# Gated linear attention and a squared-ReLU MLP: token pairs per partition for chunks ten to twenty-three

## The chip, the cores and the metric

The kernel runs on one core of a Trainium2 chip. The metric is the device time of one execution in microseconds (us); less is better. A core has TensorE (PE, matmuls and transposes), VectorE (DVE), ScalarE (ACT), GpSimd (POOL) and a queue for transfers on SyncE (SP). Each works its own instructions off in a fixed order and waits for the others through semaphores.

## The reference, cut to what matters

```python
batch, n_heads, seq, head_dim = 4, 8, 768, 48          # attention inputs q, k, v, alpha, float32
n_tokens, d_model, d_ff = 3072, 384, 2048

for t in range(S):
    state = alpha[:, :, t, :, None] * state + einsum('bhd,bhe->bhde', k[:, :, t], v[:, :, t])
    y[:, :, t] = einsum('bhd,bhde->bhe', q[:, :, t], state)
x = y.transpose(0, 2, 1, 3).reshape(B * S, H * D)      # 3072 x 384
h = maximum(x @ w_in, 0)
out = (h * h) @ w_out                                  # 3072 x 384, float32
```

alpha lies between 0.8 and 1.

## The kernel before, in words

The 3072 tokens are 24 chunks of 128, six for each batch. A chunk of the attention (below: GLA) is worked in the chunked form. ACT takes the logarithm of alpha (`L_s`), PE multiplies it with a triangle of ones (`utri_b`), which gives the running sum along the tokens, ACT exponentiates the sum with both signs (`A`, `Ainv`), and VectorE forms q·A and k·Ainv (both in `qk_s`). These two are transposed (to `qkT`). PE forms the 128x128 scores per head (`sc`), VectorE masks them while it moves them out of PSUM (`sm`), and PE adds masked scores times v (`vb`) and q·A times the carried state (`sb`). The state `st` stays in PSUM: PE adds k·Ainv times v, VectorE multiplies by the chunk's total decay (`ae_s`), ACT copies it to `sb`. The result `xn` is transposed into `xT_big`.

The MLP follows in 12 groups of chunks, most of them of two chunks. For each group PE forms w_in times x ("moe1", 48 matmuls of 256 columns for two chunks), ACT applies the ReLU (`r`), VectorE squares it (`gT`), and PE multiplies by w_out ("moe2", 16 matmuls of 384 columns per chunk). ACT or VectorE copy the result to `held`, from where it is stored.

Nothing runs in the order of the code. Each step is handed to a planner as an `Op` with an engine or a choice of engines (a dictionary with a duration for each), its dependencies and a priority. `Plan.run` places each on the engine that its durations say will finish it first, `gate` lets a chunk's running sum start only when the MLP's progress is within 3.5 to some 6.5 chunks of it, and the steps are then issued in the order of the planned starts. The order on every engine is therefore fixed when the kernel is built. Between chunks' GLA steps PE has MLP matmuls.

Three kinds of chunk exist:

- Chunks 0 to 3, two at a time (`add_super`): a partition holds two neighbouring tokens, so that the pair's load has runs of 384 bytes.
- Chunks 4 to 11 (`add_chunk` with `s < TURN`): a partition holds one token, and loads have runs of 192 bytes (`add_load`). The totals come from four one-column matmuls and two small ACT instructions (L474, L477).
- Chunks 12 to 23 (`s >= TURN`): the same, but A is written in float32 in another order (`Af`, L467), its last row is sent to `ae_s` by two small transfers on POOL's queue (L484), and q and k are transposed by one DMA on SP's queue (L515) instead of PE. From chunk 14 on, `xn` is transposed by DMA as well (`XTURN`, L414).

In `add_chunk` the products for q and k are one VectorE instruction each (L495 or L498, and L501) over 128 partitions, and POOL casts v to bfloat16 (L443). Chunks are scored one by one up to chunk 7 and two by two from chunk 8 on (`PAIRS`, `add_scores`). Loads are issued on SP's queue in chunk order; ten chunks' buffers (`LB`) are in flight. Results are stored by POOL's queue, the last three by SP's. Until the first moe2, PE also runs idle matmuls on a zero tile (`warm`) in the gaps of the plan.

Of the kernel before, what the change touches and what calls it, by code (L numbers as in the profile page):

```python
# [164 lines left out]
def kernel(  # L165
# [24 lines left out]
    srcs = [(n, a.rearrange("b h (c p) d -> b c p h d", p=P)) for n, a in srcs]  # L190
# [10 lines left out]
    LB = 10  # L201
# [27 lines left out]
    )  # L229
    utri_b = consts.tile([P, 1, P], BF16)  # L230
    nc.vector.tensor_copy(utri_b[:, 0, :], utri_f)
    half_in = consts.tile([P, P], BF16)
# [15 lines left out]
    ones_col = consts.tile([P, 1], BF16)  # L248
    nc.gpsimd.memset(ones_col, 1.0)

# [3 lines left out]
    NBUF = 4  # L254
    TURN = 12
    AE_LAT = 3.6
    L_s = big.tile([P, NBUF, H, DP], BF16)
    nc.gpsimd.memset(L_s[:, :, :, D:], 0.0)
    qk_s = big.tile([P, NBUF, 2, H, DP], BF16)
    qA_s, kI_s = qk_s[:, :, 0], qk_s[:, :, 1]  # L260
    nc.gpsimd.memset(qA_s[:, :, :, D:], 0.0)
    ident_bf = consts.tile([P, P], BF16)
    make_identity(nc, ident_bf)
    nc.gpsimd.memset(kI_s[:, :, :, D:], 0.0)
    ae_s = big.tile([P, NBUF, 2, NP], FP32)
# [26 lines left out]
    LD = 1.05  # L292
# [53 lines left out]
    SRC = dict(srcs)  # L346
    EARLY = 2 * 3
    PAIRS = 8
    XFROM, XTURN = 12, 14
# [4 lines left out]
    EITHER, SLOW = {"DVE": 0.47, "POOL": 0.95}, {"POOL": 0.95}  # L354
    KI_ON = [[EITHER, EITHER], [EITHER, EITHER]]
    ST_PRIO = -12.0
    SUP = [dict() for _ in range(NS)]

    def add_load(s, nm):
        d = C[s]  # L360
        b, c = divmod(s, NCH)
        k = s // 2

        def ld():
            if s % 2 == 0:
                PAIR[k][nm] = loads.tile([P, 2, H, D], FP32, name=nm)
            d[nm] = PAIR[k][nm][:, s % 2]
            pin(nc.sync.dma_start(out=d[nm], in_=SRC[nm][b, c]))
        prev = C[s - LB]["use_" + nm] if s - LB >= 2 * NS else None
        if 0 <= k - LB // 2 < NS:  # L370
            prev = SUP[k - LB // 2]["use_" + nm]
        d["ld_" + nm] = add("DMA", LD if s < 12 else 0.95, ld, prev, lat=2.4)

    PAIR = [dict() for _ in range(NT // 2)]
# [5 lines left out]
    def add_load2(u, nm):  # L380
        d = SUP[u]
        nm, half = nm[:2], nm[2:]
        hs = slice(HH * int(half), HH * int(half) + HH) if half else slice(0, H)

        def ld():
            if nm not in d:
                d[nm] = loads.tile([P, H, 2, D], FP32, name=nm)
            pin(nc.sync.dma_start(out=d[nm][:, hs].rearrange("p h s d -> p h (s d)"), in_=SRC2[nm][0, u][:, hs]))  # L388
        d["ld_" + nm + half] = add("DMA", LD2 / 2 if half else LD2, ld, lat=2.0, at=0.8)

# [8 lines left out]
    def add_tail(s, done, first, g):  # L399
# [23 lines left out]
        xT = add({"ACT": 0.36, "DVE": 0.27} if s < EARLY else "DVE", 0.27, e_xT, p4, prio=-9.0)  # L423
# [3 lines left out]
    def add_chunk(s):  # L427
        d = C[s]
        b, c = divmod(s, NCH)
        i = s % NBUF  # L430
        L, qA, kI, ae = L_s[:, i], qA_s[:, i], kI_s[:, i], ae_s[:, i].rearrange("p j n -> p n j")
        was = C[s - NBUF]
        old = was["end"] if s < 2 * NS + NBUF else None
        g = dict(prio=-10.0 + s * 0.01)
        last = c == NCH - 1
# [3 lines left out]
        ln = d["use_at"] = add("ACT", 0.41, e_ln, d["ld_at"], old or was["p0"], prio=-15.0 if s < EARLY else -5.0)  # L439

        def e_vb():
            d["vb"] = work.tile([P, H, D], BF16, name="vb", bufs=4)
            pin(nc.gpsimd.tensor_copy(d["vb"], d["vt"]))  # L443
        vb = d["use_vt"] = add("POOL", 0.55, e_vb, d["ld_vt"], old or was["end"], prio=-5.0)

        def e_p0():
            pm = d["pm"] = psum(p0, [P, 512], FP32)
            mm(pm[:, 0:HD], lhsT=utri_b[:, 0, :], rhs=L[:, :, 0:D], start=True, stop=True)
            for p in range(NP if s < TURN else 0):
                mm(pm[:, HD + p:HD + p + 1], lhsT=L[:, 2 * p:2 * p + 2, :], rhs=ones_col,  # L450
                   start=True, stop=True)
        p0 = Op("PE", 0.27 if s < TURN else 0.17, e_p0, [ln], takes=GLA_BANKS, lat=0.17, **g)
        p0.gla = s
        d["p0"] = p0

        def split(x, s):
            if s < TURN:
                return x.rearrange("p (h d) -> p h d", h=H)
            return x.rearrange("p (n j d) -> p n j d", n=NP, j=2)

        def e_A():
            if s < TURN:
                d["A"] = work.tile([P, H, D], BF16, name="A")
            else:
                d["Af"] = work.tile([P, 2, D, NP], FP32, name="Af", bufs=2)
                d["A"] = d["Af"].rearrange("p j d n -> p n j d")
            pin(nc.scalar.activation(d["A"], split(d["pm"][:, 0:HD], s), AF.Exp))  # L467

        def e_Ai():
            d["Ai"] = work.tile([P, H, D], BF16, name="Ainv")  # L470
            pin(nc.scalar.activation(d["Ai"], d["pm"][:, 0:HD].rearrange("p (h d) -> p h d", h=H), AF.Exp, scale=-1.0))  # L471

        def e_ae0():
            pin(nc.scalar.activation(ae[0:64, :, 0], d["pm"][0:64, HD:HD + NP], AF.Exp))  # L474

        def e_ae1():
            pin(nc.scalar.activation(ae[64:128, :, 1], d["pm"][64:128, HD:HD + NP], AF.Exp))  # L477
        plan.add(p0)
        a_ = add("ACT", 0.38 if s < TURN else 0.76, e_A, p0, **g)
        ai = add("ACT", 0.38, e_Ai, p0, after(a_), **g)  # L480

        def e_aed():
            for j in range(2):
                pin(nc.gpsimd.dma_start(out=ae_s[HF * j:HF * j + D, i, j], in_=d["Af"][P - 1:P, j]))  # L484
        if s < TURN:
            ae0 = add("ACT", 0.18, e_ae0, p0, after(ai), **g)
            p0.gives = ae1 = add("ACT", 0.19, e_ae1, p0, after(ae0), **g)
        else:
            p0.gives = ai
            ae1 = add("POOL", 1.03, e_aed, a_, lat=AE_LAT, prio=-20.0)  # L490
            ae1.dma = 0.42

        def e_qA():
            if s < TURN:
                pin(nc.vector.tensor_mul(qA[:, :, 0:D], d["qt"], d["A"]))  # L495
            else:
                v4 = "p (n j) d -> p n j d"
                pin(nc.vector.tensor_mul(qA[:, :, 0:D].rearrange(v4, j=2), d["qt"].rearrange(v4, j=2), d["A"]))  # L498

        def e_kI():  # L500
            pin(nc.vector.tensor_mul(kI[:, :, 0:D], d["kt"], d["Ai"]))  # L501
        mq = d["use_qt"] = add("DVE", 0.47 if s < TURN else 0.78, e_qA, a_, d["ld_qt"], old or was["cps"][0], **g)
        mk = d["use_kt"] = add("DVE", 0.47, e_kI, ai, d["ld_kt"], *([old] if old else [was["cps"][1], was.get("ps")]), **g)

        def e_p1q():
            d["pT"] = psum(p1q, [P, 2 * NP, P], BF16)
            for p in range(NP):
                tr(d["pT"][:, p, :], qA[:, 2 * p:2 * p + 2, :], ident_bf)

        def e_p1k():  # L510
            for p in range(NP):
                tr(d["pT"][:, NP + p, :], kI[:, 2 * p:2 * p + 2, :], ident_bf)
        def e_turn():
            d["qkT"] = work.tile([P, 2 * NP, P], BF16, name="qkT")
            pin(nc.sync.dma_start_transpose(out=d["qkT"], in_=qk_s[:, i].rearrange("p x h d -> p (x h d)")))  # L515
        if s < XFROM:
            p1q = plan.add(Op("PE", 0.22, e_p1q, [mq], takes=GLA_BANKS, **g))
            p1k = plan.add(Op("PE", 0.22, e_p1k, [mk, after(p1q)], lat=0.15, **g))

        def e_cp(lo, hi):  # L520
            if lo == 0:
                d["qkT"] = work.tile([P, 2 * NP, P], BF16, name="qkT")
            cast(cpk if lo else cp, d["qkT"][:, lo:hi, :], d["pT"][:, lo:hi, :])
        if s < EARLY:
            cp = add({"ACT": 0.49, "DVE": 0.34}, 0, lambda: e_cp(0, NP), p1q, **g)
            cpk = add({"DVE": 0.34, "ACT": 0.49}, 0, lambda: e_cp(NP, 2 * NP), p1k, after(cp, -9.0), **g)
        elif s < XFROM:
            cp = cpk = add("DVE", 0.61, lambda: e_cp(0, 2 * NP), p1k, was["py_op"], **g)
        else:
            cp = cpk = add("XB", 0.0, e_turn, mq, mk, was["py_op"], lat=2.8)  # L530
            cp.turn = 1.2
        if s < XFROM:
            p1q.gives = cpk

        d.update(cps=[cp, cpk], mk=mk, vb_op=vb, ae1=ae1, kI=kI, ae=ae)
        if s < PAIRS:
            add_scores(s, 1)
            add_back(s)
        elif s % 2:
            add_scores(s - 1, 2)  # L540
            add_back(s - 1)
            add_back(s)
# [429 lines left out]
    for x in DMA_ORDER + [s for s in range(2 * NS, NT) if s not in DMA_ORDER]:  # L972
# [7 lines left out]
        else:  # L980
            for nm, _ in srcs:
                add_load(x, nm)
# [85 lines left out]
```

## Time and profile before

| what | value |
|---|---|
| median of three runs (lowest, highest) | 179.01 us (178.74, 179.09) |
| the profiled execution: its time, its span | 179.8 us, 178.1 us |
| granted TensorE clock in it | 0.999 |
| VectorE: the squares `gT` | 96, 46.1 us busy, mean 514 ns |
| VectorE: the masks `sm` from `sc` and from a bank | 24 of 684 ns, 16 of 681 ns |
| VectorE: q·Af, q·A, k·Ainv | 12 of 854 ns, 8 of 565 ns, 20 of 548 ns |
| ACT: the ReLUs | 96, mean 611 ns |
| ACT: Af, A, Ainv | 12 of 883 ns, 8 of 495 ns, 20 of 514 ns |
| POOL: casts to `vb` of chunks 4 to 23 | 20, 553 ns (507 the usual one) |
| POOL: transfers of `ae_s` and of results | 24 of 511 ns, 17 of 545 ns |
| loads of q, k, alpha, 192 KB each | 24 each, 3.8 to 4.0 us from issue to landing |
| DMA transposes `qkT` and `xT_big` | 12 and 10, 4.4 and 4.0 us to landing |

The profile is one execution. Its span runs from the first to the last instruction, and the time of the execution lies 1.7 us above it. A busy time counts an instruction from start to end; neighbours on an engine can overlap, so the pace of an engine is read from start to start. TensorE's ends are modelled. DMA engines were busy nearly without a break until 150 us. The two last groups' MLP work fills PE from 155 us to 175 us; the last store ends the span.

### The profile page before, as it was taken

The page shows a single profiled execution, that of the slowest core. Times are in us where ns is not written, and L with a number is a line of the kernel's source. Part 1 is how long each engine was busy: PE and PEld are TensorE (multiplying, and loading weights), DVE is VectorE, ACT ScalarE, POOL GpSimd, SP SyncE. Part 2 cuts the span into 40 slices and gives each one's busy share as a digit, 9 for nine tenths or more (in the row PEclk, how much of TensorE's full clock was granted, in tenths as well). Part 3 has the DMA queues.
Part 4 walks back from the last instruction along what each step waited for, and adds up shares of the span by engine and source line. Part 5 has one row for each costly group of instructions (what it writes and reads, how often), then busy time and mean ns, then how long its engine had stood idle before and what let it go on. Part 6 is the DMA issues. An engine that isn't in the chain of part 4 may idle for free.

```text
span 178.1 us, 4801 instructions
## 1 busy us (share of the span) xinstructions
PE 172.0 (97%) x1866; PEld 126.3 (71%) x1867; DVE 124.8 (70%) x256; ACT 122.8 (69%) x263; POOL 53.1 (30%) x95
## 2 busy tenths in 40 slices
PE   7999999999999999999999999899999999999993
PEld 3567684566896788878766786686688867757862
DVE  6699769936799798998986976798248933800600
ACT  4557789456898689979956698874598947522821
POOL 6023467711110211115222233327736080212000
PEclk9999999999999999999999999999999999999999
DMA  5999999999998999988999799999999969232012
GB/s 128 275 271 322 311 352 377 247 194 213 216 185 156 213 184 203 229 176 155 125 214 209 144 209 109 187 193 239 212 204 294 211 162 212 69 91 89 0 44 88
DMA packets 115798, 34.34 MB, mean 193 GB/s; under 512 B 109840, under 2 KB 114064, under 8 KB 115776
## 3 DMA queue, kind: packets, MB, share of 16 engines
q1 hardware_dynamic: 113536, 29.89, 81.5%
q0 software_dynamic: 2240, 4.15, 7.3%
q8 instruction: 14, 0.23, 0.6%
q14 instruction: 8, 0.07, 0.1%
HBM read 25.17 MB, written 4.72 MB: 168 GB/s over the span
## 4 chain that ended last, share of the span: by engine, by line
PE 79%; DMA 7%; DVE 4%; SPq 3%; ACT 3%; issue 1%; ACTq 0%; DVEq 0%
PE bank L273 71%; PE bank L276 4%; SPq L388 3%; DMA qt<-in_q_dram 3%; DMA at<-in_alpha_dram 3%; PE sc L273 2%; PE st L273 2%; DMA kt<-in_k_dram 2%; ACT r L878 1%; DVE sm L570 1%; ACT Af L467 1%; DVE qkT L395 1%; ACT xn L393 0%; DVE sm L763 0%; DVE xT_big L395 0%
## 5 line engine op out<-in xcount | busy, mean ns | idle before, releaser
L273 PE MATMUL bank<-xT_big,w_in_b 128*128 128x256 bf16 (+2 forms) x599 | 72.0, 268 | 0.3 <-ACT r L878 0.2
L273 PE MATMUL bank<-w_out_b,gT 128*128 128x384 bf16 (+2 forms) x400 | 69.8, 319 | 0.0
L878 ACT ACTIVATE r<-bank 128x512 bf16<-128x512 f32 x96 | 57.0, 611 | 13.5 <-PE bank L273 11.5
L886 DVE TENSOR_TENSOR gT<-r 128x512 bf16<-128x512 bf16 x96 | 46.1, 514 | 23.7 <-ACT r L878 23.4
L273 PEld LDWEIGHTS <-w_in_b 128*128 128x128 bf16 x600 | 53.2, 98 | 11.2 <-issue 1.1
L273 PEld LDWEIGHTS <-gT 128*128 128x128 bf16 x400 | 37.1, 98 | 19.4
L443 POOL CAST vb<-vt 128x384 bf16<-128x384 f32 x20 | 11.1, 553 | 58.1 <-DMA vt<-in_v_dram 30.8
L953 ACT COPY held<-bank 128x384 f32<-128x384 f32 x22 | 10.6, 481 | 14.9 <-PE bank L273 14.6
L484 POOL DMA_DIRECT2D ae_s<-Af x24 | 12.2, 511 | 25.4 <-ACT Af L467 22.2
L570 DVE TENSOR_TENSOR sm<-sc,utri_b 128x512 bf16<-128x512 f32 x24 | 15.4, 684 | 2.0 <-PE sc L273 1.8
L273 PEld LDWEIGHTS <-qkT 64*128 64x128 bf16 (+2 forms) x304 | 10.5, 97 | 5.1 <-issue 2.4
L393 ACT CAST xn<-bank 128x384 bf16<-128x384 f32 x24 | 11.1, 485 | 4.4 <-PE bank L273 4.1
L498 DVE TENSOR_TENSOR qk_s<-qt,Af 128x384 bf16<-128x384 f32 x12 | 10.2, 854 | 4.6 <-ACT Af L467 4.6
L438 ACT ACTIVATE L_s<-at 128x384 bf16<-128x384 f32 x20 | 10.6, 543 | 2.7 <-DMA at<-in_alpha_dram 2.7
L961 POOL DMA_DIRECT2D out_dram<-held x17 | 9.2, 545 | 7.9 <-ACT held L953 7.9
L467 ACT ACTIVATE Af<-bank 128x384 f32<-128x384 f32 x12 | 10.6, 883 | 0.9 <-PE bank L273 0.7
L501 DVE TENSOR_TENSOR qk_s<-kt,Ainv 128x384 bf16<-128x384 f32 x20 | 11.0, 548 | 0.0
L395 DVE COPY qkT<-bank 128x1024 bf16<-128x1024 bf16 (+1 forms) x14 | 8.3, 609 | 3.4 <-PE bank L276 3.4
L609 ACT CAST sb<-st 128x384 bf16<-128x384 f32 x16 | 8.0, 499 | 3.9 <-DVE st L604 3.8
L471 ACT ACTIVATE Ainv<-bank 128x384 bf16<-128x384 f32 x20 | 10.3, 514 | 0.0
L570 DVE TENSOR_TENSOR sm<-bank,utri_b 128x512 bf16<-128x512 f32 x16 | 10.2, 681 | 0.0
L604 DVE TENSOR_TENSOR st<-st,ae_s 128x384 f32<-128x384 f32 x16 | 8.9, 557 | 1.7 <-PE st L273 1.7
(71 smaller groups left out, 165.6 us busy)
## 6 DMA issues: line engine op xcount, KB each, us to landing
at<-in_alpha_dram SPq DMA_DIRECT2D x24, 192.0 KB, 4.0
qt<-in_q_dram SPq DMA_DIRECT2D x24, 192.0 KB, 3.8
kt<-in_k_dram SPq DMA_DIRECT2D x24, 192.0 KB, 4.0
vt<-in_v_dram SPq DMA_DIRECT2D x20, 192.0 KB, 3.9
out_dram<-held POOLq DMA_DIRECT2D x17, 192.0 KB, 4.5
wo<-in_moe_w_out_dram SPq DMA_DIRECT2D x4, 768.0 KB, 7.3
wi<-in_moe_w_in_dram SPq DMA_DIRECT2D x4, 384.0 KB, 6.8
wi<-in_moe_w_in_dram SPq DMA_DIRECT2D x2, 768.0 KB, 5.6
```

The lines of the kernel that those rows point to most:

```text
L273: pin(nc.tensor.matmul(*a, **kw))
L393: pin(nc.scalar.copy(out_t, in_t))
L438: pin(nc.scalar.activation(L[:, :, 0:D], d["at"], AF.Ln))
L443: pin(nc.gpsimd.tensor_copy(d["vb"], d["vt"]))
L467: pin(nc.scalar.activation(d["A"], split(d["pm"][:, 0:HD], s), AF.Exp))
L471: pin(nc.scalar.activation(d["Ai"], d["pm"][:, 0:HD].rearrange("p (h d) -> p h d", h=H), AF.Exp, scale=-1.0))
L484: pin(nc.gpsimd.dma_start(out=ae_s[HF * j:HF * j + D, i, j], in_=d["Af"][P - 1:P, j]))
L501: pin(nc.vector.tensor_mul(kI[:, :, 0:D], d["kt"], d["Ai"]))
L570: pin(nc.vector.tensor_mul(d["sm"][:, hh], d["sc"][hh], utri_b.to_broadcast([P, NP, P])))
L878: pin(nc.scalar.activation(box["r"][:, 0:w], box["ph"][:, 0:w], AF.Relu))
L886: pin(nc.vector.tensor_mul(gT[g][:, f0:f0 + per, lo * P:lo * P + n], r, r))
L953: pin(nc.scalar.copy(box["ob"], box["po"]))
```

## The change: token pairs from chunk ten on

Chunks 4 to 9 keep their form (`add_single`). Chunks 10 to 23 become seven pairs (`add_pair`), pair 5 to pair 11. A pair loads 256 tokens at once, two neighbouring tokens per partition, with runs of 384 bytes; its four loads replace eight. Partitions 0 to 63 hold the pair's first chunk, 64 to 127 the second.

- `pr` is the product of the two tokens' alphas, by VectorE or POOL. One Ln and one matmul with `half_in` (a triangle of ones for each half of the partitions) give the running sum at every odd token of both chunks; four two-column matmuls give both totals.
- The even token's A is A of the odd one divided by its alpha. VectorE takes the reciprocal of alpha (`rec`) and q's even half is multiplied by it in place; k's even half is multiplied by alpha in place (VectorE or POOL).
- Score matmuls want one chunk's 128 tokens on 128 partitions: even tokens on partitions 0 to 63, odd ones on 64 to 127. So each of q·A and k·Ainv is written by four products of 64 partitions (`e_mul`). The two with s equal to ab stay on their partitions, and may run on POOL; the other two read one half of the partitions and write the other, on VectorE. The casts to `vb` are split in the same way (POOL where the partitions stay, else ACT or VectorE).
- `mask_b` replaces `utri_b` for these chunks, since tokens stand in another order.
- The totals go to `ae_s` by ACT, as in the early chunks; `Af` and the POOL transfers L484 go.
- Two DMA transposes per pair (q, k), from pair 5 on (chunks 10 and 11 had PE transposes before); `xn` is transposed by DMA from chunk 10 on (before: 14).
- Results of these chunks come out in that token order. For the last two groups the ReLU undoes it by writing with a step of two elements (`NATURAL`); for chunks 10 to 19 each result is stored by two transfers.
- Chunks 8 and 9 are scored one by one. Buffers for eight chunks instead of ten, three `qk_s` pair buffers, another gate.

In the order of the changed kernel, of the pairs' products POOL has 7 of q, 7 of k, 5 of `pr` and 4 of the in-place products of k; VectorE has 21 of q, 21 of k, 7 reciprocals, 7 in-place products of q, 3 of k, 2 of `pr`, and 9 of the 14 casts that change partitions.

```diff
-    LB = 10
+    LB = 8
+            nc.gpsimd.tensor_copy(mask_b[h, 0, HF * t:HF * t + HF], (sutri_f if ab > t else utri_f)[h, h])
-    TURN = 12
-    PAIRS = 8
-    XFROM, XTURN = 12, 14
+    PAIRS = 6
+    XFROM, XTURN = 10, 10
+    NS1 = NS + 3
+    def add_load(u, nm):
...
+            d[nm] = loads.tile([P, H, 2, D], FP32, name=nm)
+            pin(nc.sync.dma_start(out=d[nm].rearrange("p h s d -> p h (s d)"), in_=SRC2[nm][b, c]))
+        free = U[u - UB]["use_" + nm] if u >= UB else []
...
+    def add_pair(u):
...
+        pr = [add(scaled({"DVE": 0.47} if early else EITHER, part), 0, lambda v=v: e_prod(pr[v], v), ld("at", v), *(prev["ln"] if prev else []),
+                  prio=-16.0 if early else -5.0) for v in range(n)]
+            pin(nc.scalar.activation(L[:, hv[v], 0:D], d["pr"][:, hv[v]], AF.Ln))
...
+            pin(nc.vector.reciprocal(d["rec"][:, hv[v]], d["at"][:, hv[v], 1]))
...
+            mul(op, d["qt"][:, hv[v], 0], d["qt"][:, hv[v], 0], d["rec"][:, hv[v]])
...
+            mul(op, d["kt"][:, hv[v], 0], d["kt"][:, hv[v], 0], d["at"][:, hv[v], 1])
...
+        d["use_at"] = pr + rec + k0
+
+        def e_vb(op, s, ab):
+            r, o = slice(HF * ab, HF * ab + HF), slice(HF * s, HF * s + HF)
...
+            cast(op, d["vb"][o, ab], d["vt"][r, :, s])
...
+            e = {"POOL": 0.55} if s == ab else {"ACT": 0.42, "DVE": 0.30}
...
+            mm(pm[:, 0:W], lhsT=half_in, rhs=L[:, hv[v], 0:D], start=True, stop=True)
+            if v == n - 1:
+                for p in range(NP):
+                    mm(pm[:, HD + 2 * p:HD + 2 * p + 2], lhsT=L[:, 2 * p:2 * p + 2, :], rhs=both, start=True, stop=True)
...
+        def e_mul(op, dst, nm, f, s, ab):
+            r, o = slice(HF * ab, HF * ab + HF), slice(HF * s, HF * s + HF)
+            mul(op, dst[o, ab, :, 0:D], d[nm][r, :, s], d[f][0][r])
...
+                for s in range(2):
+                    ops.append(add(EITHER if s == ab else {"DVE": 0.47}, 0,
+                                   lambda a=(dst, nm, f, s, ab), ops=ops, j=len(ops): e_mul(ops[j], *a), *deps, prio=-10.0 + u * 0.02 + ab * 0.01))
...
+                pin(nc.sync.dma_start_transpose(out=d["qkT"][:, x].rearrange("p t n c -> p (t n) c"),
+                                                in_=qk_s[:, i, x].rearrange("p t h d -> p (t h d)")))
...
+    NATURAL = range(NG - 2, NG)
...
+            o = box["r"][:, 0:w].rearrange("p (a c t) -> p a t c", t=2, c=HF) if g in NATURAL else box["r"][:, 0:w]
+            i = box["ph"][:, 0:w].rearrange("p (a t c) -> p a t c", t=2, c=HF) if g in NATURAL else box["ph"][:, 0:w]
+            pin(nc.scalar.activation(o, i, AF.Relu))
...
-            return s <= (LEAD if s < 10 else min(6.5, LEAD + 0.3 + 0.3 * (s // 2 * 2 - 10)) + 0.5 * (s % 2)) + (prog["m1"] + prog["m2"]) / 5.12
+            return s <= (3.5 if s < 8 else min(6.5, 3.5 + 0.2 * (s - 6))) + (prog["m1"] + prog["m2"]) / 5.12
```

## The prediction

> **What bounds the kernel now.** I read the page's busy times first, then who waited for whom on PE, then the timeline of PE and of VectorE.
>
> ```profile
> span 178.1 us, 4801 instructions
> PE 172.0 (97%) x1866; PEld 126.3 (71%) x1867; DVE 124.8 (70%) x256; ACT 122.8 (69%) x263; POOL 53.1 (30%) x95
> ```
>
> ```profile
> PE bank L273 <- DVE both L236: 1.1, 1, 1.1
> PE bank L276 <- DVE qk_s L700: 0.4, 1, 0.4
> PE bank L273 <- ACT r L878: 0.4, 2, 0.2
> ```
>
> The first lines show an almost gapless PE; the waits (total, times, longest) show that PE waited 2.4 us in all, most of it in the first 25. But busy PE need not be PE at its peak, so I read its starts:
>
> ```profile
> 123.65 0.81 PE L273 MATMUL bank<-w_out_b,gT 128*128 128x384 bf16 x4
> 124.30 0.33 PE L273 MATMUL bank<-sb,qkT 128*128 128x96 bf16 x4
> 124.47 0.36 PE L273 MATMUL bank<-vb,sm 128*128 128x48 bf16 x8
> 124.67 0.32 PE L273 MATMUL bank<-L_s,utri_b 128*128 128x384 bf16 x1
> 124.83 3.41 PE L273 MATMUL bank<-w_out_b,gT 128*128 128x384 bf16 x20
> ```
>
> From start to start: eight 48-column matmuls 0.20 us, four of 384 columns 0.65 (0.162 each), four of 96 columns 0.17. PE goes from one to the next without a hole, so **the sum of PE's work sets the time**: a shorter DMA, ACT or VectorE instruction gains nothing by itself, though DMA is full until 150 us. PE's order is fixed, so an engine that comes late stops PE at once.
>
> **VectorE's pace** is needed for that. Its rows:
>
> ```profile
> 71.38 0.55 DVE L604 TENSOR_TENSOR st<-st,ae_s 128x384 f32<-128x384 f32 x1
> 71.85 0.54 DVE L495 TENSOR_TENSOR qk_s<-qt,A 128x384 bf16<-128x384 f32 x1
> 72.31 0.55 DVE L501 TENSOR_TENSOR qk_s<-kt,Ainv 128x384 bf16<-128x384 f32 x1
> ...
> 74.69 0.78 DVE L886 TENSOR_TENSOR gT<-r 128x512 bf16<-128x512 bf16 x2
> 75.39 1.28 DVE L570 TENSOR_TENSOR sm<-sc,utri_b 128x512 bf16<-128x512 f32 x2
> 76.59 1.28 DVE L570 TENSOR_TENSOR sm<-bank,utri_b 128x512 bf16<-128x512 f32 x2
> ```
>
> Start to start, a product of 384 columns takes 0.47, a square gT 0.35, a mask sm 0.60: less than their durations, since neighbours overlap.
>
> **The port.** The squares last 418 ns in the median but 514 in the mean and 1682 at most. The long ones lie under GpSimd's casts; these are the lines of POOL and of VectorE in one window (start, us, instruction, count, idle time before):
>
> ```profile
> 27.16 1.66 POOL L322 CAST w_out_b<-wo 128x1536 bf16<-128x1536 f32 x1 [1.00 <-DMA wo<-in_moe_w_out_dram]
> 29.39 1.70 POOL L322 CAST w_out_b<-wo 128x1536 bf16<-128x1536 f32 x1 [0.57 <-DMA wo<-in_moe_w_out_dram]
> 31.50 1.53 POOL L322 CAST w_out_b<-wo 128x1536 bf16<-128x1536 f32 x1 [0.41 <-DMA wo<-in_moe_w_out_dram]
> 33.68 1.62 POOL L322 CAST w_out_b<-wo 128x1536 bf16<-128x1536 f32 x1 [0.65 <-DMA wo<-in_moe_w_out_dram]
> ```
>
> ```profile
> 27.72 7.85 DVE L886 TENSOR_TENSOR gT<-r 128x512 bf16<-128x512 bf16 x9 [0.23 <-ACT r L878]
> ```
>
> Nine squares take 7.85 us instead of 9 x 0.35 = 3.2: 4.7 us lost to 6.5 us of casts, 72%. Over the kernel, 96 x (514 - 418) = 9.2 us are lost to 25.0 us of casts (the five cast groups of POOL by line), 37%. The Trainium skill, SBUF — State Buffer, "SBUF: two separate sides", says why: VectorE instructions with two SBUF inputs and GpSimd instructions that read SBUF share a port pair that one of them holds for its whole instruction. The trace agrees: masks and state products, which read PSUM, do not lengthen. By that rule every product that the change puts on GpSimd speaks against it.
>
> **The change part by part.** Counts are from the changed kernel's instruction order.
>
> PE. Gone: 16 transposes of qk_s (chunks 10, 11) and 12 of xn (chunks 10 to 13), at 0.056 (eight in 0.45, three in 0.17 in the chain): 1.57. Cumulative sums: 14 matmuls of 384 columns become 7: 7 x 0.162 = 1.13. Added: 28 two-column matmuls for the totals, less 8 one-column ones, at the 0.025 of a 48-column one: 0.5. Net **-2.2 us**, all of it on the path. Scores, state, output and both MoE products keep their counts, and the first 45 us of PE's order stay all but the same.
>
> DMA. 56 loads of 192 KB become 28 of 384 KB with runs twice as long; 24 tiny POOL transfers of ae_s go; output stores of ten chunks split in two (18 POOL issues of 0.53 more, late). Since PE does not wait for loads now, I count nothing. The cover is the prefetch of four pairs; without it a pair's load costs some 4 us (the median landing). On SP's queue 28 loads of 0.57 go (16 us) and 2 transposes of qkT and 4 of xT at about 1.7 come (10 us), each transpose in front of the loads behind it. A load now also waits until pr, the reciprocal and k0, on POOL or VectorE, have read the tile of four pairs before, and the transposes queued behind it wait too; that costs nothing unless those engines are a whole pair late.
>
> ACT. Per pair one Ln (0.54) and one Ainv (0.51) go and two Af (0.88) become one A (0.50); two exps of 0.17 per pair and five casts in all come. About 1.9 us per pair less, and no gain, as ACT does not hold PE.
>
> VectorE. Gone: 14 products for q (12 of 0.78 by starts, 2 of 0.47), 14 for k (0.47), 2 qkT copies (0.60), 7 xT copies (0.29): 20 us. Added: 42 half-partition products (as many columns each, so 0.47), 7 reciprocals, 7 + 3 + 2 more products, 9 casts to vb, a held copy: 32 us. The trace has no reciprocal: between 0.35 (the shortest copy of 384 columns) and 0.85 (the slowest row, qk_s<-qt,Af); I take the product's 0.47. The 64-partition cast lies between 0.19 (64x64 cast) and 0.47; I take 0.35.
>
> The order also pushes the pairs together. From the scores of pair 5 to those of pair 10 PE has 192 + 124 MoE matmuls (0.109 from 48 in 5.23; 0.162) = 41.0, five sums 0.8, totals 0.5, 68 of 96 columns 2.9, 80 of 48 columns 2.1, scores 5 x 0.55 = 2.7: **50.0 us**. The same prices give 74.9 for before's scores from 74.64 to 151.31, which took 76.7; scaled by that, 51.2. VectorE has, between the masks of the same pairs: 38 squares 13.3, 35 products 16.5, 20 masks 12.0, 9 state products 4.2, 4 reciprocals 1.9, 8 casts 2.8, 2 held copies 1.0: **51.7 us**. In before's stretch it was busy 56.5 of 76.7 us, 74%. So VectorE is full here before any port is lost.
>
> GpSimd then reads SBUF in the same stretch with 18 products (pr, q, k) and 10 casts. A cast is 0.507 undisturbed; a product has no row: between 0.51 (a cast) and 1.01 (two inputs, each as dear as a cast); I take 1.0, as both inputs must be read. 18 + 5.1 = 23 us. VectorE's loss: from 5.3 (cheap products, 14.2 us at 37%) to 16.6 (72%); VectorE's instructions that read no second SBUF input are 19 of 51.7 us, so pure chance would give 63%. I take 45%, 10.4 us, since a pair's q and k products stand on both engines at once but casts often meet masks.
>
> Products that start at other partitions than their neighbours: no row shows it; from nothing to 0.08 each (duration 0.55 less pace 0.47), 28 of them: 0 to 2.3; I take 1.0. The Trainium skill, VectorE: DVE Perf Modes, "Two Vector instructions with no wait between them", says that an instruction whose start quadrant differs from the last one's waits until the earlier ones have finished; it would make this 2.3, and no run shows it yet.
>
> Sum: 51.7 + 10.4 + 1.0 = 63.1 against 51.2, so VectorE is 11.9 late at pair 10's scores. Cover: in before, the last q/k transpose lands 2 to 3 us ahead of its scores (issued 85.07, landing after 4.4, scores at 91.79): 2.5. Stall 9.4; with PE's -2.2, **+7.2**. Behind pair 10, VectorE has 6.5 us of work for 12.9 of PE, so nothing is added, but PE's lost time does not return.
>
> The sum stands against the profiled execution (179.8 us, span 178.1); the median of the runs is 179.0, so I add the difference to that: **186.2 us**. Ends: 51.7 + 5.3 - 51.2 - 2.5 = 3.3 of stall, 180.1 in all; 51.7 + 16.6 + 2.3 - 51.2 = 19.4 without cover, 196.2.
>
> **Rivals.**
> - VectorE keeps up (faster). If GpSimd's products fall under masks and state products, or their port use is short, VectorE ends within the 2.5 us of cover and PE's sum alone counts: 179.0 - 2.2 = 176.8. It decides below about 2 us lost. For it: the window 70 to 80 us, where VectorE was busy 9.87 of 10 us and PE did not wait. Against it: the ledger, full before any loss.
> - The strided relu (about even). The last two groups' relus write every second element. Af, with steps of 16 bytes, took 883 ns where A took 495; were this so here, a relu would take 611 + 512 x (388/384) = 1128. Eight of them are 9.0 us against 5.2 of moe1; three banks and the remaining moe2 cover all but some 1.5 us per group: 176.8 + 3 = 179.8. The Trainium skill, SBUF — State Buffer, "Door 1: The DMA port swizzle", says that steps are free while two elements share a 16-byte line, which fits Af and would make this rival nothing.
> - Worse: a reciprocal above 0.85, or products on GpSimd above 1.01: past 195.
>
> That PE's work does not shrink is excluded by the order's counts.
>
> **Chances.** VectorE bound 0.62 (186.2, own range 180 to 195), VectorE keeps up 0.26, relu 0.07 (half within, half slower), worse 0.05. 0.2%, 0.36 us, is about what a measurement here can tell from no change. Faster 0.26, within 0.04, slower 0.70. The range runs from 176.4 to 195.0: it leaves out the worse case and tails of two others.
>
> **What would show it.** Right: PE waits of several us for sm, qkT or gT between 65 and 130 us, VectorE at 95% there, squares and products stretched beside POOL products of about 1 us. Wrong: PE without waits and a span of 176; POOL products near 0.5 us; a wait on loads; or stalls only after 150 us, under relus near 1.1 us.

## The result and the profile after

| | before | after |
|---|---|---|
| median (lowest, highest), four runs each, same chip | 179.05 us (178.74, 179.09) | 217.4 us (217.09, 218.09) |
| ratio, 95% interval | | 1.215 (1.212 to 1.219) |
| span of the profiled execution | 178.1 us | 215.4 us |
| granted TensorE clock | 0.999 | 0.952 |

Slower, as forecast, but by 38.4 us and not by 7.2. Where some runs of a kernel took over 1.5% more than its fastest, the median given is that of the others. The page of the changed kernel: span, busy times, and the rows of VectorE and of PE's clock in 40 slices of 5.4 us.

```profile
span 215.4 us, 4796 instructions
...
PE 179.3 (83%) x1852; PEld 127.8 (59%) x1852; DVE 165.2 (77%) x290; ACT 117.7 (55%) x259; POOL 74.3 (35%) x110
...
DVE  4898896769999999939999999969999945325000
...
PEclk9999999999999999579999969588899999999999
```

PE has 14 matmuls fewer and is idle 36 us (6 before). VectorE stands at 9 from the 10th slice to the 32nd with two short breaks, and its zeros at the end are the last groups' MLP work, in which PE alone is busy. The clock falls in slices that follow a stall of PE. Who PE waited for (total, times, longest):

```profile
PE bank L274 <- ACT ae_s L533: 8.2, 1, 8.2
PE st L274 <- DVE qk_s L410: 5.6, 3, 3.0
PE bank L274 <- ACT r L1039: 5.2, 5, 1.9
PE bank L274 <- DVE sm L718: 2.6, 5, 1.4
```

The list names ACT first, though ACT is busy 55%. The timelines around 85 us show what stood behind it: VectorE, then ACT, then PE (start, us, instruction, count, idle time before).

```profile
80.88 1.26 DVE L410 TENSOR_TENSOR qk_s<-qt,A 64x384 bf16<-64x384 f32 x1
82.17 3.01 DVE L410 TENSOR_TENSOR qk_s<-kt,Ainv 64x384 bf16<-64x384 f32 x3
85.21 2.55 DVE L483 RECIPROCAL rec<-at 128x384 f32<-128x384 f32 x1
87.68 0.36 DVE L1047 TENSOR_TENSOR gT<-r 128x512 bf16<-128x512 bf16 x1
```

```profile
88.16 0.60 ACT L1039 ACTIVATE r<-bank 128x512 bf16<-128x512 f32 x1 [7.25 <-DVE gT L1047]
88.95 0.60 ACT L1039 ACTIVATE r<-bank 128x512 bf16<-128x512 f32 x1 [0.20 <-DVE gT L1047]
89.45 0.16 ACT L533 ACTIVATE ae_s<-bank 64x8 f32<-64x8 f32 x1
```

```profile
81.94 0.22 PE L274 MATMUL bank<-qkT 64*128 64x128 bf16 x1
90.34 0.58 PE L274 MATMUL bank<-qkT 64*128 64x128 bf16 x7 [8.18 <-ACT ae_s L533]
91.47 0.48 PE L274 MATMUL st<-vb,qk_s 128*128 128x96 bf16 x4 [0.55 <-ACT sb L760]
91.75 3.90 PE L274 MATMUL bank<-w_out_b,gT 128*128 128x384 bf16 x16
```

VectorE works products and a reciprocal, so a square comes late; the ReLU that needs that square's buffer waits 7.25 us at the head of ACT's queue; the tiny `ae_s` behind it, long ready, would free the bank that PE's next scores need. So an ACT wait is VectorE's lateness, passed on by a fixed order. After it, 16 matmuls of 384 columns take 3.90 us, 0.24 each in place of 0.162: the clock has dropped.

The groups of VectorE that matter (busy, mean ns):

```profile
L483 DVE RECIPROCAL rec<-at 128x384 f32<-128x384 f32 x7 | 17.8, 2544 | 0.1
L410 DVE TENSOR_TENSOR qk_s<-qt,A 64x384 bf16<-64x384 f32 x21 | 16.8, 802 | 0.5
L410 DVE TENSOR_TENSOR qk_s<-kt,Ainv 64x384 bf16<-64x384 f32 x21 | 16.1, 765 | 0.3
```

A reciprocal takes 2.54 us, five times what I had priced; the split products last some 0.78 in the mean, against 0.55 for a whole one before.

### The profile page after: what moved, and what is told of

It is laid out like the page before. It is cut to its first block, busy times and chain, and to the rows that moved or that the text cites. A ratio compares the mean times of both kernels' runs of the same rounds, so it can differ in the third digit from the quotient of the medians.

```text
span 215.4 us, 4796 instructions
## 1 busy us (share of the span) xinstructions
PE 179.3 (83%) x1852; PEld 127.8 (59%) x1852; DVE 165.2 (77%) x290; ACT 117.7 (55%) x259; POOL 74.3 (35%) x110
## 4 chain that ended last, share of the span: by engine, by line
PE 46%; DVE 28%; issue 16%; ACT 5%; POOL 4%; POOLq 0%; DVEq 0%; ACTq 0%
PE bank L274 41%; DVE qk_s L410 10%; DVE rec L483 5%; DVE gT L1047 3%; DVE sm L718 3%; PE bank L277 2%; DVE vb L419 2%; ACT r L1039 2%; POOL qk_s L410 1%; POOL vb L421 1%; PE st L274 1%; DVE sm L919 1%; DVE qt L410 1%; DVE st L754 1%; PE sc L274 1%
## 5 line engine op out<-in xcount | busy, mean ns | idle before, releaser
L1047 DVE TENSOR_TENSOR gT<-r 128x512 bf16<-128x512 bf16 x96 | 46.5, 523 | 10.0 <-ACT r L1039 9.5
L1126 POOL DMA_DIRECT2D out_dram<-held x28 | 14.7, 530 | 24.7 <-ACT held L1114 24.7
L410 DVE TENSOR_TENSOR qk_s<-qt,A 64x384 bf16<-64x384 f32 (+1 forms) x27 | 20.3, 752 | 2.5 <-ACT A L649 2.0
L421 POOL CAST vb<-vt 64x384 bf16<-64x384 f32 x14 | 8.6, 617 | 35.1 <-PE bank L274 34.6
L410 DVE TENSOR_TENSOR qk_s<-kt,Ainv 64x384 bf16<-64x384 f32 (+1 forms) x27 | 19.7, 728 | 0.3
L410 POOL TENSOR_TENSOR qk_s<-qt,A 64x384 bf16<-64x384 f32 x7 | 8.7, 1240 | 30.2 <-ACT A L524 17.6
L483 DVE RECIPROCAL rec<-at 128x384 f32<-128x384 f32 x7 | 17.8, 2544 | 0.1
L274 PE MATMUL st<-vb,qk_s 128*128 128x96 bf16 (+1 forms) x96 | 7.7, 211 | 10.6 <-DVE qk_s L410 5.6
L274 PEld LDWEIGHTS <-qk_s 128*128 128x128 bf16 (+1 forms) x96 | 5.4, 99 | 13.3 <-DVE qk_s L410 6.7
L718 DVE TENSOR_TENSOR sm<-sc,mask_b 128x512 bf16<-128x512 f32 x14 | 9.0, 682 | 4.5 <-PE sc L274 4.4
L274 PE MATMUL bank<-vb,sm 128*128 128x48 bf16 (+1 forms) x224 | 10.2, 186 | 2.3 <-DVE sm L718 2.3
L274 PEld LDWEIGHTS <-sm 128*128 128x128 bf16 (+1 forms) x224 | 8.5, 98 | 4.2 <-DVE sm L718 2.7
```

Of the source, the lines that this page charges most:

```text
L274: pin(nc.tensor.matmul(*a, **kw))
L410: pin((nc.gpsimd if op.eng == "POOL" else nc.vector).tensor_mul(out_t, a, b))
L421: pin(nc.gpsimd.tensor_copy(out_t, in_t))
L483: pin(nc.vector.reciprocal(d["rec"][:, hv[v]], d["at"][:, hv[v], 1]))
L718: pin(nc.vector.tensor_mul(d["sm"][:, hh], d["sc"][hh], d.get("mask", mask_b).to_broadcast([P, NP, P])))
L1047: pin(nc.vector.tensor_mul(gT[g][:, f0:f0 + per, lo * P:lo * P + n], r, r))
```

## Experiments

Theory A: the reciprocal is what makes it so slow. Theory B: the port, that is GpSimd's products. Later theories: C, VectorE's total work sets the end, whatever it is for; D, the fixed order of ACT and PE and PE's lower clock hold the time; F, the length of the one chain from load to scores counts. Every ratio is to the kernel before on the same chip.

**E1, the reciprocal as a product** (even tokens' q then lacks the division).

```diff
-            pin(nc.vector.reciprocal(d["rec"][:, hv[v]], d["at"][:, hv[v], 1]))
+            pin(nc.vector.tensor_mul(d["rec"][:, hv[v]], d["at"][:, hv[v], 1], d["at"][:, hv[v], 1]))
```

> The reciprocal of alpha is replaced by a product of alpha with itself, on VectorE, in the same place and with the same planned duration, so that every engine's order stays; the even tokens' q is wrong by that. In the changed kernel's trace a reciprocal takes 2544 ns, a product 0.47 by starts: 7 x 2.07 = 14.5 us of VectorE less. Theory A (the reciprocal and what queues behind it make over half of the 38.4 us): at most 196 us. Theory B (the port shared with GpSimd's products makes over half, the reciprocal costs its own time and no more): 203 us or above.

Measured 206.6 us, ratio 1.150 (1.147 to 1.153): 10.8 us go, and 26.9 stay over the 179.7 that the kernel before took on this chip. B's range is met, not A's: the reciprocal is a part of the loss, and less than half of it.

**E2, all products on VectorE**, in the same order.

```diff
-        pin((nc.gpsimd if op.eng == "POOL" else nc.vector).tensor_mul(out_t, a, b))
+        pin(nc.vector.tensor_mul(out_t, a, b))
```

> All 23 products that the planner gave to GpSimd are issued on VectorE instead, at the same planned starts; the reciprocals stay. VectorE gains 23 x 0.47 = 10.8 us of work and loses the waits for GpSimd's products (its half-partition products last 784 ns in the mean where 548 was the undisturbed row: 42 x 0.235 = 9.9 us). Theory A (reciprocal): 212 to 223 us, no great change. Theory B (port): below 203 us.

Measured 216.4, ratio 1.205 (1.201 to 1.210): A's range, and nearly no change, which could mean that the port costs nothing, or that VectorE's additional products cost what the port did.

**E3, both edits.**

> Both edits: product in place of the reciprocal, and no product on GpSimd; the even tokens' q is wrong. Theory A: within 4 us of the run with the reciprocal replaced alone. Theory B: at least 10 us below that run. If VectorE's work alone, without any lost port, is too much for the order (51.7 of 51.2 us between the scores of pairs 5 and 10, and 8.5 us more with these products), it stays above 185 us in either case.

Measured 203.6, ratio 1.133 (1.129 to 1.136). With neither reciprocal nor shared port 24 us remain. But VectorE has GpSimd's 23 products on top now, so this run alone does not tell the port's price from theirs; E11 does.

**E4, the reciprocal on ACT**, as exp(-ln(alpha)), planned anew.

```diff
-            pin(nc.vector.reciprocal(d["rec"][:, hv[v]], d["at"][:, hv[v], 1]))
+            pin(nc.scalar.activation(d["rec"][:, hv[v]], d["at"][:, hv[v], 1], AF.Ln))
...
+            pin(nc.scalar.activation(d["rec"][:, hv[v]], d["rec"][:, hv[v]], AF.Exp, scale=-1.0))
```

> The reciprocal is made by ScalarE as exp(-ln(alpha)), two instructions of about 0.5 us per pair, with the right result; VectorE has no reciprocal. The planner places things anew. Theory A: within 4 us of the run with the product in its place, or lower, since VectorE also loses that product's 0.47. Theory B: above 200 us.

Measured 204.1, ratio 1.136 (1.131 to 1.141). It computes the whole reference and is 13 us better than the change.

**E5, disputed rows alone**, in a program of their own that ran once.

> A row of single instructions in place of the kernel; it leaves the whole computation out and stores ones. It gives the disputed prices alone, start to start. If products that start at other partitions than their neighbours cost nothing extra, eight of 64 partitions that stay, cross or alternate all run at 0.47; if each waits for the last one's end, the alternating ones run at 0.55 to 0.57 and those that all start alike at 0.47. Reciprocal: 2.4 to 2.6 each. GpSimd product of 64 partitions: 0.9 to 1.0 alone. Beside GpSimd products, 20 VectorE products lengthen by 40 to 100% of the GpSimd time (the port theory), 12 masks do not, and reciprocals do not (one input). The ReLU with a step of two elements: 1.1 us if the strided-ReLU rival holds, 0.6 if steps of 4 bytes within a line are free.

The timelines of VectorE and of POOL, where six GpSimd products run beside 20 products, 12 masks and 6 reciprocals in turn:

```profile
29.59 10.31 DVE L65 RECIPROCAL rc<-src 128x384 f32<-128x384 f32 x4
...
58.48 15.35 DVE L48 TENSOR_TENSOR dst<-src,fac 128x384 bf16<-128x384 f32 x20
...
74.75 8.67 DVE L98 TENSOR_TENSOR smo<-ps,msk 128x512 bf16<-128x512 f32 x12
...
84.33 15.49 DVE L108 RECIPROCAL rc<-src 128x384 f32<-128x384 f32 x6
```

```profile
58.33 6.81 POOL L73 TENSOR_TENSOR p_dst<-p_src,p_fac 64x384 bf16<-64x384 f32 x6
...
74.47 5.81 POOL L73 TENSOR_TENSOR p_dst<-p_src,p_fac 64x384 bf16<-64x384 f32 x6
...
84.06 5.80 POOL L73 TENSOR_TENSOR p_dst<-p_src,p_fac 64x384 bf16<-64x384 f32 x6
```

A reciprocal is 2.58 from start to start, alone (10.31/4) and beside GpSimd (15.49/6). GpSimd products take 0.97 beside masks and reciprocals and 1.14 beside products. Of the 20 products, the first six start 1.18 apart and the rest 0.59: one GpSimd product delays VectorE by one product, 0.59. So the port theory holds for VectorE's products, which have two SBUF inputs, and not for masks, which read PSUM, or for reciprocals, which have one input. Here each product writes the tile of the last one and waits for it (0.58 to 0.59 each for all patterns), so the price of other start partitions is not seen here. The strided ReLU:

```profile
L114 ACT ACTIVATE rs<-ps 128x512 bf16<-128x512 f32 x4 | 2.9, 737 | 0.1
L112 ACT ACTIVATE ro<-ps 128x512 bf16<-128x512 f32 x4 | 2.4, 597 | 98.5 <-DVE ro L29 98.4
```

737 ns against 597: neither the rival's 1128 nor nothing.

**E6, two products of 128 partitions per operand in place of four of 64**, with E3's edits.

```diff
-            r, o = slice(HF * ab, HF * ab + HF), slice(HF * s, HF * s + HF)
-            mul(op, dst[o, ab, :, 0:D], d[nm][r, :, s], d[f][0][r])
+            if s == ab:
+                mul(op, dst[:, ab, :, 0:D], d[nm][:, :, s], d[f][0])
```

> The kernel with both edits (product for the reciprocal, all products on VectorE), and in addition each operand of a pair written by two products of 128 partitions in place of four of 64; so the scores' operands hold the tokens of the wrong chunk, and even tokens' q lacks the division. It takes 28 VectorE instructions out, 28 x 0.565 = 15.8 us, in the same order otherwise. Theory C (VectorE has more work than the stretch has time): 183 to 190, against 203.6 with both edits alone. Rival D (the fixed order on ACT and PE, and PE's lower granted clock after gaps, hold the time and not VectorE's sum): 198 or more.

Measured 186.3, ratio 1.036 (1.033 to 1.040): 17.3 us less than E3, as C says; D's 198 is refuted.

**E7, the four products kept, but none crosses partitions**, with E3's edits.

```diff
-            r, o = slice(HF * ab, HF * ab + HF), slice(HF * s, HF * s + HF)
+            r = o = slice(HF * s, HF * s + HF)
```

> The kernel with both edits, and the four products of 64 partitions kept, but reading and writing the same partitions (so half of the operands hold the wrong tokens). Counts and order are unchanged. If reading one half of the partitions and writing the other is what costs, some 28 x 0.10 = 2.8 us go: 200 to 201. If the price lies in the neighbours' different starts (0 and 64), which stay, nothing changes: 203 to 204.

Measured 201.6, ratio 1.121 (1.117 to 1.125), between the two. The trace decides by the time from one q or k product to the next after 60 us. In E3, 6 of 41 take 0.47 to 0.48 and 33 take 0.55 to 0.59; in E7, 16 take 0.47 to 0.48 and 25 take 0.55 to 0.59; in E6 all 17 take 0.46 to 0.48. In E7 products with equal starts often follow each other, in E3 hardly ever. The partitions that each product reads and writes, taken from the two kernels' instruction orders, sort the times: where neighbours read from the same start and write to the same start, 16 of 16 take 0.47 to 0.48 in E7 and 6 of 7 in E3; where one of the two starts differs, 25 of 25 in E7 and 33 of 34 in E3 take 0.55 to 0.59. Five of E3's six short ones cross partitions, behind one that crosses in the same way. E3's and E6's timelines of VectorE:

```profile
76.64 1.68 DVE L410 TENSOR_TENSOR qk_s<-qt,A 64x384 bf16<-64x384 f32 x3 [0.15 <-ACT A L524]
...
79.49 2.27 DVE L410 TENSOR_TENSOR qk_s<-kt,Ainv 64x384 bf16<-64x384 f32 x4
```

```profile
95.98 1.01 DVE L410 TENSOR_TENSOR qk_s<-kt,Ainv 128x384 bf16<-128x384 f32 x2
```

Three take 1.68 and four 2.27: each starts when the last one ends. Of the two whole ones the second starts 0.46 after the first. So it is the start that differs from the neighbour's that costs 0.09, and reading one half and writing the other costs nothing by itself. The rule of the Trainium skill that the prediction weighed (VectorE: DVE Perf Modes, "Two Vector instructions with no wait between them") agrees with this.

**E8, a constant lead of 3.5 chunks in the gate**, with E4's edit.

```diff
-            return s <= (3.5 if s < 8 else min(6.5, 3.5 + 0.2 * (s - 6))) + (prog["m1"] + prog["m2"]) / 5.12
+            return s <= (3.5 if s < 8 else min(3.5, 3.5 + 0 * (s - 6))) + (prog["m1"] + prog["m2"]) / 5.12
```

> The reciprocal worked by ACT as exp(-ln(alpha)) as before (204.1), and the running sums let go by a constant lead of 3.5 chunks over the MLP's progress in place of one that grows to 6.5; so the pairs are not pushed together, and VectorE has the same work over a longer stretch with more MLP matmuls beside it. Theory C: 188 to 198. Rival D, in which the lateness comes from single waits in the fixed order: within 2 of 204.

Measured 207.5, ratio 1.155 (1.151 to 1.159): worse, and neither expectation met. VectorE's work is unchanged, but it is idle 13 us longer (34.7 after 60 us, 22.1 in E4). Letting pairs start later made things wait; it did not spread the work.

**E9, copies in place of the squares** (`tensor_copy` at L1047; the MLP lacks its square).

> The changed kernel with each of the 96 squares replaced by a plain copy of the ReLU's result (the MLP is then without its square); the reciprocals, the split products and GpSimd's share stay. A copy has one SBUF input and should take some 0.2 in place of 0.34 to 0.52. Theory C (VectorE's sum over the stretch sets the end, whatever the instructions are for): between the scores of pair 5 and pair 10 43 squares of 17.1 us become some 8.6, before it and behind it 2 to 3 us more: 204 to 209 against 217.4. Rival F (the length of one chain counts: load, reciprocal, split products, transposes, scores; the squares are not in it): 214 or more.

Measured 211.6, ratio 1.176 (1.169 to 1.183). The squares are in no chain to the scores, so F is refuted (214 or more); but the gain is 5.8 and not 8 to 13. A copy took 0.35 us in the mean, not 0.2: 0.29 for the 85 that meet no cast or product of GpSimd, 0.82 for the 11 that do, so an instruction with one SBUF input is not safe from it either. VectorE's work fell by 9.3 us after 60 us, of which 3.8 came back as its idle time, 3.2 of them in front of copies that waited for a ReLU. The time misses C's range as well.

**E10, fewer pairs** (`NS1 = NS + 5`, then `+ 7`), with E4's edit.

> The reciprocal worked by ACT (204.1 with seven pairs), and pairs only from chunk fourteen on: five pairs in place of seven, chunks 10 to 13 in the form of chunks 4 to 9. If each pair costs the same, (204.1 - 179.0)/7 = 3.6 each: 197. Theory C, in which VectorE has a quarter of its time to spare before a pair costs anything: 184 to 194.

> As before it, with pairs only from chunk eighteen on, three of them. If each pair costs the same: 190. Theory C: 178 to 186, since chunks 4 to 17 leave VectorE slack and only the last three pairs exceed it.

Measured 195.4 (1.087, 1.081 to 1.093) with five pairs and 187.1 (1.040, 1.034 to 1.047) with three. Both lie 1.4 and 1.1 us beyond C's range and within 3 of a constant price per pair, so these two did not tell the expectations apart.

**E11, GpSimd's products as fills that read nothing** (0.9 in place of the products).

```diff
-        pin((nc.gpsimd if op.eng == "POOL" else nc.vector).tensor_mul(out_t, a, b))
+        pin(nc.gpsimd.memset(out_t, 0.9) if op.eng == "POOL" else nc.vector.tensor_mul(out_t, a, b))
```

> The changed kernel with each product that GpSimd has (pr, k in place, the unmoved quarters of q and k) replaced by a fill of the same tile with 0.9, which reads nothing; so these tiles do not hold the products. VectorE's list and both engines' order stay, reciprocals too. By the trace, VectorE's instructions between pair 5 and pair 10 are about 8 us longer than in the kernel with both edits (28 products by 0.18, 43 squares by 0.04, 8 casts by 0.13). Theory B (that is the port, and GpSimd's share costs what it takes there): 207 to 211 against 217.4. If these lengths hide in VectorE's waits: 214 or more. Theory A' (GpSimd's products are late themselves, and PE waits for them): below 205.

Measured 203.8, ratio 1.140 (1.136 to 1.145): 13.6 us less, in the range of A' and above B's size. But the mechanism is B's: VectorE's work after 60 us (defined below) falls from 116.8 to 103.7 with the same instructions, which is all but 0.5 of the gain. My 8 us counted only the stretch between pair 5 and pair 10. It also explains E2: the port took 13 us, and 23 products more on VectorE take as much (116.7 less 103.7 us of work).

**All kernels on one line.** For each I added, over VectorE's instructions from 60 us on, the time from start to end or to the next start, whichever comes first ("work"; the last one is left out).

| kernel | work, us | median, us | median less work |
|---|---|---|---|
| E6 whole products | 85.4 | 186.3 | 100.9 |
| E10 three pairs | 86.7 | 187.1 | 100.4 |
| E10 five pairs | 95.7 | 195.4 | 99.7 |
| E7 none crosses | 101.7 | 201.6 | 99.9 |
| E3 both | 103.5 | 203.6 | 100.1 |
| E11 fills | 103.7 | 203.8 | 100.1 |
| E4 reciprocal on ACT | 103.7 | 204.1 | 100.4 |
| E1 reciprocal as product | 105.6 | 206.6 | 101.0 |
| E2 all on VectorE | 116.7 | 216.4 | 99.7 |
| after | 116.8 | 217.4 | 100.6 |
| E9 copies | 107.5 | 211.6 | 104.1 |
| E8 constant lead | 103.3 | 207.5 | 104.2 |
| before | 76.6 | 179.0 | 102.4 |

Ten kernels with 85 to 117 us of work lie within 0.7 us of time = 100.4 + work. Their granted clocks run from 0.952 to 1.000 without a trace of it in the last column. The last column is, by its making, the first 60 us, VectorE's idle time after them, the time from VectorE's last instruction to the end, and the 1.7 us outside of the span. So the table says that VectorE's idle time (19 to 23 us) and that end (15 to 17 us) hardly change in these ten while its work changes by 31. E9 lies above by the idle time that it added; E8 added 13, but its time behind VectorE's last instruction is 10 shorter (7.0 against 17.4 in E4).

**E12, the kernel before with more VectorE work**: in chunks 10 to 23 the product for k (L501 of before) formed two, three and five times. VectorE idled 20 of 76.7 us in the stretch that the prediction took from this kernel; the line leaves it almost nothing to spare.

> The kernel before, in its own order, with the product for k formed twice in chunks 10 to 23: 14 VectorE instructions more, 0.47 to 0.58 each, 6.6 to 8.1 us. If time follows VectorE's work one for one here too: 185 to 187. Rival S (before has some 20 us of VectorE time to spare): 179 to 180.5.

> The same with the product three times: 28 more, 13 to 16 us. One for one: 191 to 195. Rival S: 179 to 183.

> The same with the product five times: 56 more, 26 to 33 us. One for one: 204 to 212. Rival S, with 20 us hidden and the rest paid: 186 to 195.

Measured 181.4 (1.011, 1.007 to 1.015) with 84.3 us of work, 187.9 (1.043, 1.031 to 1.054) with 90.2, and 204.4 (1.134, 1.122 to 1.146) with 106.6. The second's waits of PE, which had hardly any before:

```profile
PE st L273 <- DVE sm L571: 2.6, 1, 2.6
PE bank L276 <- DVE xT_big L395: 1.3, 1, 1.3
PE bank L273 <- DVE sm L571: 1.1, 2, 0.7
```

The third lies in the one-for-one range; the first two lie below that and above S, so neither expectation holds throughout. Median less work is 97.1, 97.7 and 97.8, so before's order hides about the first 5 us (179.0 - 97.8 - 76.6 = 4.6) and then pays one for one. At equal work it is some 3 us better than the change's order.

## Why the prediction was wrong

Right: the sign; VectorE as the engine that holds PE; PE's counts; the squares and products stretched beside POOL products of about 1 us (0.95 alone, 1.04 to 1.24 in the kernel). Of the signs, VectorE was busy 94% from 60 to 130 us, close to the 95% named; but PE's longest waits were put down to `ae_s` and to `qk_s` for the state, and those for sm and gT came to some 2.5 us each. Wrong was the size. The stretch that I worked out, between the scores of pair 5 and of pair 10, now runs from 81.7 to 164.0 us. Its window of the changed kernel (length; busy us of PE, weight loads, VectorE, ACT, POOL; clock):

```profile
81.70:164.00 82.30, 59.78 (x571) 42.11 (x571) 75.89 (x124) 38.27 (x87) 28.02 (x36) 0.88 0.61 133
```

VectorE has 75.9 us of work where I forecast 63.1, and idles 6.4 where I forecast none; 82.3 in all. The window between the same scores in E6:

```profile
76.60:135.30 58.70, 53.57 (x570) 39.00 (x569) 53.13 (x118) 37.98 (x87) 12.40 (x22) 0.97 0.94 190
```

Without reciprocals and GpSimd's products, and with half of the split products, VectorE's 53.1 us of work still exceeds the 51.2 that I gave PE (PE is busy 53.6 there, at a granted clock of 0.97).

Term by term for the 75.9:

- **The reciprocal is the mis-sized term**: "between 0.35 (the shortest copy of 384 columns) and 0.85 (the slowest row, qk_s<-qt,Af); I take the product's 0.47". It is 2.48 to its successor's start. Five lie in the stretch (I counted four), 12.4 us in place of 1.9: +10.5. No row of before was a division, and rows of products and copies are no bound for one. The ends of the forecast, 180.1 and 196.2, both keep the 0.47. E1 and E4 show its worth: 10.8 and 13.3 us.
- The port: 8.7 in the stretch (28 split products 5.4, squares 1.8, casts 1.2, others 0.3, by the lengths of E11), forecast 10.4 and range 5.3 to 16.6. Right.
- Start partitions: 0.09 each, 2 to 2.5 in the stretch, forecast 1.0 and range 0 to 2.3.
- Squares: 43 in the stretch, not 38: +1.9. One product more and longer casts: +0.9.

**The second failure is the frame of the sum.** "Cover: ... 2.5" took VectorE to be on time at pair 5, and "Behind pair 10 ... nothing is added" took the loss to end there. Pair 5's scores came at 81.7, 5.1 us later than in E6; PE had waited 5.5 us since 55 us, against 0.1 in before. From 66 to 82 us VectorE was already full, with a reciprocal and nine split products of 0.84. Pair 11 came 15.6 us behind pair 10, where PE's work is 12.9. The sum from the start of the pairs: 5.5 + (82.3 - 51.2) + 2.7 = 39.3 on top of 176.8 gives 216.1 of the measured 217.4. That is 29.9 more than the forecast stall of 9.4: 12.8 of VectorE's work in the stretch (10.5 of it the reciprocals), 6.4 of its idle time there, 8.2 outside of the stretch, and the 2.5 of cover.

**The third is what "busy 56.5 of 76.7 us, 74%" was taken for.** VectorE idled 20 us in before's stretch, and by setting its work against PE's time as if it need never idle, I let the added work fill them. E12 shows that, with products at the place where E12 adds them, only about 5 us could be filled: in E12's largest case VectorE still idles 26.7 us after 60 us, and PE waits some 15 us for its results. Idle time in front of a ReLU's result is not spare time for work that stands in another place of a fixed order.

The rivals: VectorE keeps up (0.26) was refuted at once; the strided ReLU (0.07) was not it: PE runs without a wait from 169.6 to the end, over those ReLUs. "Worse: a reciprocal above 0.85" was what came, and so did its other condition, GpSimd products above 1.01; it had a chance of 0.05.

What stays open: whether a plan made with the right prices would hide more. No kernel with pairs here beats the one before; the best of them with the whole computation is three pairs at 187.1. Even E6, which has products for reciprocals, none of the pairs' products on GpSimd and half of the split ones, takes 186.3.

## What to carry to other kernels

When an edit moves work to an engine that is 70 to 75% busy in a fixed order, test for the slack before counting on it: repeat one of its instructions a few dozen times and see from which dose on the end moves; here about 5 us of 20. Price an operation that the trace doesn't show by measuring it alone, or keep the range open upward. And splitting an elementwise instruction by partitions doubled its cost here: a product lasts 0.55 us over 64 partitions and 0.56 over 128 (E5). Neighbours that start at other partitions add 0.09 each to that (E7).

## What the runs showed of the hardware

- A reciprocal of 128x384 float32 on VectorE takes 2.54 us in the kernel and 2.55 alone; its 2.48 to the next start are 5.3 products of the same shape (0.47).
- Neighbouring VectorE products that read from or write to other start partitions do not overlap: 0.56 in place of 0.47 (E3, E7).
- Beside a GpSimd product, VectorE's products and GpSimd's alternate one by one (1.18 us a round), while masks from PSUM and reciprocals are untouched (E5). Plain copies of 128x512 are not: 0.82 us beside GpSimd's work, 0.29 else (E9).
- After the 8.2 us stall of PE the granted clock was 0.80 in the window from 90 to 100 us. The Trainium skill (TensorE: Matmul & The Clock Gate, "HAM oscillation — how this bites in real kernels") warns of idle gaps of PE beyond some 3.4 us; the trace agrees for this one. But the clock also fell behind waits of 2.55 and 2.95 us (0.59 from 124 to 128 us, 0.50 from 136 to 140), so here shorter gaps were not safe. The table above shows no cost of it, since VectorE sets the pace.
